# Fused SSM convolution and 32-head attention: another order of projections, shifts and loads in the setup

## The chip, the cores and the metric

One core of one Trainium2 chip runs the whole program in one launch. The metric is device time in microseconds (us), the median of the runs; smaller is better. Engines are named as the profile names them: PE (TensorE matmul), PEld (its weight loads), DVE (VectorE), ACT (ScalarE), POOL (GpSimd), SP (SyncE, which here only issues DMAs).

## The reference

Two unrelated halves, each from an input of 2048 positions by 576 channels, are joined along the channels.

```python
# half a: a diagonal state-space convolution, 576 channels with 128 complex modes each
dt = exp(log_dt); P = exp(dt * A * l)            # A = A_re + i A_im, l = 0..2047
K  = real(einsum("dn,dnl,dn->dl", C, P, dt * B))
a  = irfft(rfft(pad(u)) * rfft(pad(K)))[:2048] + u * Dskip
# half b: attention, 32 heads of 18, one key and one value head shared by all
q = x @ wq; k = x @ wk; v = x @ wv
p = softmax(q k^T * 18**-0.5); o = p v; b = o @ wo
out = concatenate([a, b], axis=-1)
```

## The kernel before

**Attention.** Positions are cut into four chunks of 512 columns (`CT`), keys and queries alike. Transposed scores are made for a pair of heads at a time: a step of the main loop takes one pair, one query chunk and one block of 128 keys. Two matmuls (`scores`, L470) write a tile `s` of 128 x 1024, one ACT instruction (`exponentials`, L478) turns it into `P`, and four matmuls per two of these (`product`, L768) add `P` times the values (`v_sb`) into the bank `ops`. There are 1024 such exponentials. The loop takes them in threes (`NS` = 3 banks of `s`).

The two operands of `scores` are augmented: `kaug` holds, for each key, 18 rows of the rounded key, 18 of its rounding rest, 18 of the rounded key again and a row of ones; `aug` holds for each of a pair of heads the rounded query twice, its rest, and a row (54 or 118) with minus a bound of the scores, so that the exponential needs no maximum. The bound comes from the largest absolute key and query entries: a reduction (`km`, `ab`), a small matmul with `spread` (`kmx`), a product (`aw`), a matmul with `sel` (`up`), a maximum (`un`), and `sh`, which a DMA carries into the row.

Queries come in five groups of output columns per chunk (`MQ`; m = 0 to 4). Group (0, 0) is projected in the setup. The others are projected in pieces between the steps (`qproj`, L347), stored to DRAM (`qd`) by POOL's queue, and fetched by SP as `aug` tiles, five of them in a ring.

**The state-space half** (`Conv`) runs beside it: twelve groups of 48 channels, each with a front (exponentials, sines, tables made by DVE, a matmul `kg`) and a back (transforms by matmuls with `dft`, products on DVE). `arguments` prepares for a group the phases `f`, `r` (cosine and sine) and the exponents `m`; ACT takes the sines and the exponential of them, between two loads of its function table, and DVE multiplies both with `m` (L1072, L1074). In the setup `begin` lets the first group run twelve pieces ahead, up to these two products.

**Order.** PE, ACT and DVE run in the order in which the program writes them. A planner in `main` (class `Clock`, `fill`) writes it: it keeps a model of the engines' times and puts side work (query projections, output projections, transforms) between the steps while a credit lasts. SP's and POOL's orders are set by the scheduler of the language; eight semaphores are used in turn for the DMAs of SP and ACT together, eight for POOL's, so a DMA waits until the eighth before it has landed.

**The setup**, the place of the change. SP loads for each of the five 128-row pieces k of x first the part of chunk 0 (`x0`) and then that of the three other chunks (`xr`). PE projects, piece by piece, the keys of all four chunks into one bank (`kps`, one strip of 32 rows each) and the first query group into another (`q0_0`), then the values (`vps`). Then come the rounding, the DMAs into `kaug` (`place`, chunk by chunk) and `aug` (L405), the bound, the shift row (L444), the other groups' key maxima (`kmx4`), and the values turned by four transposes (`vp`). Only then `main` writes its first scores.

Of the kernel before, what the change touches and what calls it, by code (L numbers as in the profile page):

```python
# [9 lines left out]
F32 = mybir.dt.float32  # L10
# [174 lines left out]
class Attention:  # L185
# [36 lines left out]
    def setup(self, tp, conv):  # L222
# [9 lines left out]
        spread = tp.tile([P, 140], F32, name="spread_sb")  # L232
# [6 lines left out]

        keys = cp.tile([P, 5, CT], F32R, tag="oT", name="keys")  # L240
        kh, kl, vt = keys[:, 0, :], keys[:, 1, :], keys[:, 2, :].bitcast(F32)
        self.q0 = keys[:, 3, :], keys[:, 4, :]
        ident = tp.tile([P, P], F32, name="ident")
        km = tp.tile([P, 5], F32, name="km")
# [4 lines left out]

        def load(q, k):  # L250
            n = DT[k][1]
            q.dma_start(x0[:n, k, :], a["xT"][0, :n, k, :])
            q.dma_start(xr[:n, k], a["xT"][1:4, :n, k, :].rearrange("c p n -> p c n"))
# [8 lines left out]
        nc.scalar.dma_start(spread, a["sel"][:, 45:185])  # L262
        nc.gpsimd.dma_start(ident, a["ident"])
        for b in (54, 118):
            nc.gpsimd.dma_start(self.kaug[b:b + 1, :], a["ones"])
        V.memset(self.v[:, :, DH:], 1.0)
        self.ubound, self.first = None, True
        self.aug = {n: self.ring[n % NAUG] for n in range(64)}
        self.ready, self.od, self.qd = set(), {}, {}
# [4 lines left out]
        conv.begin()  # L274
        kps, self.qps = (self.ps_s.tile([P, 2, CT], F32, tag="s", name=n)[:, 0, :] for n in ("kps", "q0_0"))
        pv = self.ps_o.tile([P, CT], F32, tag="o", name="vps")

        def project(ps, j, k):
            for c in range(NCH):
                nc.tensor.matmul(ps[32 * c:32 * c + 32, :], wkv[:, k, j:j + 32], xr[:, k, c - 1, :] if c else x0[:, k, :],  # L280
                                 start=(k == 0), stop=(k == 4), tile_position=(0, 32 * c))
# [3 lines left out]
        for k in range(2):  # L285
            project(pv, 32, k)
        nc.scalar.activation(kh, kps, AF.Copy)
# [11 lines left out]
        for k in range(2, 4):  # L299
            project(pv, 32, k)  # L300
        self.side_work = side = Stream(self.side(), self.k, 99.0)
        while self.first:
            side.advance()
# [1151 lines left out]
```

## Time and profile before

| | |
|---|---|
| median of 3 runs | 1211.45 us (1211.01 to 1211.5) |
| profiled execution | span 1211.2 us from its first to its last instruction |
| PE | 1142.3 us busy (94%) |
| ACT | 1032.6 us (85%), of which 967.8 in 1024 exponentials |
| DVE | 977.2 us (81%) |
| first exponential of a score | starts at 32.79 us |

Busy times of engines overlap and don't add up. The profile's chain of waits follows the work that ended last back from the end; its shares say through which engine the end was reached. Times in the text are from the start of the span. The runs list no separate time for the profiled execution: the median lies 0.25 us above its span.

### The profile page before, as it was taken

To read this page: it belongs to the slowest core of one execution; us is meant where nothing else is said; L and a number is where in the kernel's file an instruction comes from. 1 tells how busy PE (TensorE), PEld (TensorE's weight loads), DVE (VectorE), ACT (ScalarE), POOL (GpSimd) and SP (SyncE) were. 2 spreads that over 40 slices of the span, in tenths; PEclk is the share of its full clock that TensorE was granted. 3 is DMA by queue.
4 is the path that set the end of the run, shared out by engine and by line. 5 is a ranking of instruction groups with operands and counts; after the bars stand their busy time and mean duration, and the time that the engine had idled before them with its cause. 6 is when DMAs were issued, how large, how long until landed. Compare 5 with 4: busy or idle time off the path is not lost.

```text
span 1211.2 us, 32889 instructions
## 1 busy us (share of the span) xinstructions
PE 1142.3 (94%) x13852; PEld 469.4 (39%) x13852; DVE 977.2 (81%) x1564; ACT 1032.6 (85%) x1091; POOL 118.6 (10%) x210
## 2 busy tenths in 40 slices
PE   5999899999899999999998999999999999999997
PEld 1443333343333344334443333444434334334332
DVE  4769978978997978988877988976997995895823
ACT  2788989888889888898987999888999988988983
POOL 2221210210310000010320000010240000000000
PEclk9899999999999999999999999999999999999999
DMA  7442333122343111223323122122143112012111
GB/s 228 146 138 91 100 106 102 52 82 79 108 134 106 36 65 62 81 80 103 107 71 117 40 92 93 35 81 84 52 132 121 47 36 90 26 51 79 35 41 42
DMA packets 61713, 102.15 MB, mean 84 GB/s; under 512 B 17692, under 2 KB 28570, under 8 KB 61048
## 3 DMA queue, kind: packets, MB, share of 16 engines
q1 hardware_dynamic: 47046, 85.32, 21.2%
q0 software_dynamic: 13824, 14.07, 4.5%
q8 instruction: 111, 1.82, 0.6%
q10 hardware_dynamic: 690, 0.60, 0.2%
q14 instruction: 42, 0.34, 0.1%
HBM read 55.66 MB, written 42.89 MB: 81 GB/s over the span
## 4 chain that ended last, share of the span: by engine, by line
PE 73%; DVE 11%; ACT 8%; issue 3%; DMA 3%; SPq 0%; POOL 0%; ACTq 0%; DVEq 0%
PE ops L768 30%; PE s L470 22%; ACT P L478 8%; PE q L347 5%; PE op L182 4%; PE iy L182 3%; PE kg L1139 3%; DVE acc L112 2%; DMA xr<-xT 2%; DVE ks L112 1%; DVE tab L112 1%; PE hu L182 1%; PE hk L182 1%; PE lu L182 1%; PE lk L182 1%
## 5 line engine op out<-in xcount | busy, mean ns | idle before, releaser
L478 ACT ACTIVATE P<-s 128x1024 f32<-128x1024 f32 x1024 | 967.8, 1031 | 144.7 <-PE s L470 139.9
L768 PE MATMUL ops<-P,v_sb 128*32 128x512 f32 x4096 | 515.4, 599 | 5.6 <-DVE o L116 5.3
L470 PE MATMUL s<-aug,kaug 55*128 55x512 f32 x2048 | 364.0, 442 | 23.8 <-ACT P L478 21.4
L470 PEld LDWEIGHTS s<-aug,kaug 55*128 55x128 f32 x2048 | 169.1, 185 | 331.9 <-ACT P L478 301.1
L768 PEld LDWEIGHTS ops<-P,v_sb 128*32 128x32 f32 x4096 | 114.2, 110 | 155.3 <-issue 120.4
L412 POOL DMA_DIRECT2D qd<-qh x116 | 66.4, 578 | 403.4 <-DVE qh L116 403.4
L347 PE MATMUL q<-x,wq_sb 128*32 128x256 f32 x1360 | 85.7, 389 | 2.9 <-DVE ob L116 1.5
L182 PE MATMUL op<-wo_sb,oT 126*32 126x288 f32 (+1 forms) x1144 | 82.9, 410 | 4.8 <-DVE ob L116 4.1
L112 DVE TENSOR_TENSOR tab<-tab,tt 128x576 f32<-128x576 f32 (+1 forms) x72 | 59.1, 821 | 1.7
L347 PEld LDWEIGHTS q<-x,wq_sb 128*32 128x32 f32 x1360 | 41.1, 111 | 48.0 <-issue 18.6
L112 DVE TENSOR_TENSOR tab<-sum,r 128x576 f32<-128x576 f32 (+1 forms) x72 | 58.7, 816 | 0.0
L112 DVE TENSOR_TENSOR tab<-r,dif 128x576 f32<-128x576 f32 (+1 forms) x72 | 58.7, 816 | 0.0
L112 DVE TENSOR_TENSOR tt<-f,sum 128x576 f32<-128x576 f32 (+1 forms) x72 | 58.7, 816 | 0.0
L112 DVE TENSOR_TENSOR tab<-tab 128x576 f32<-128x576 f32 (+1 forms) x72 | 58.6, 814 | 0.0
L182 PEld LDWEIGHTS op<-wo_sb,oT 126*32 126x32 f32 (+1 forms) x1144 | 32.3, 109 | 50.9 <-issue 18.9
L116 DVE COPY ksb<-kg 128x192 f32<-128x192 f32 x48 | 17.4, 363 | 42.0 <-PE kg L1139 41.7
L112 DVE TENSOR_TENSOR acc<-acc,pt 128x1728 f32<-128x1728 f32 (+2 forms) x36 | 48.6, 1350 | 0.4
L112 DVE TENSOR_TENSOR pt<-us,ks 128x1728 f32<-128x1728 f32 (+2 forms) x36 | 48.0, 1349 | 0.1
L450 POOL DMA_DIRECT2D qd<-sh x19 | 11.8, 619 | 353.6 <-DVE sh L120 353.5
L1139 PEld LDWEIGHTS kg<-tab 128*32 128x32 f32 x2304 | 36.4, 110 | 23.5 <-issue 8.5
L182 PE MATMUL iy<-w,dft_sb 128*32 128x192 f32 x768 | 38.5, 337 | 7.0 <-DVE ql L112 5.9
L112 DVE TENSOR_TENSOR u<-u,iy 128x384 f32<-128x384 f32 x24 | 13.2, 551 | 37.0 <-PE iy L182 36.8
(134 smaller groups left out, 1000.5 us busy)
## 6 DMA issues: line engine op xcount, KB each, us to landing
aug<-qd SPq DMA_DIRECT2D x124, 110.0 KB
od<-o SPq DMA_DIRECT2D x31, 256.0 KB
fr<-stage SPq DMA_DIRECT2D x10, 624.0 KB
qd<-qh POOLq DMA_DIRECT2D x24, 216.0 KB, 4.5
u<-u SPq DMA_DIRECT2D x12, 384.0 KB
kd<-ksb SPq DMA_DIRECT2D x12, 384.0 KB
kt<-kd SPq DMA_DIRECT2D x48, 96.0 KB
outa<-u SPq DMA_DIRECT2D x12, 384.0 KB
```

What stands on the lines that cost most here:

```text
L112: return self.v.tensor_tensor(out, *a, **k)
L116: return self.v.tensor_copy(out, *a, **k)
L182: nc.tensor.matmul(ps[j:e], w[:, j:e], x, start=start, stop=stop, tile_position=(0, j))
L347: nc.tensor.matmul(ps[o, 256 * f:256 * f + 256], w[:, k, i], xt[:, k, x], start=(k == 0), stop=(k == 4), tile_position=(0, 32 * j))
L412: q.dma_start(qd[h:h + n, row + d:row + d + nd, cs], src[i1:i1 + n * nd, :cs.stop - cs.start].bitcast(F32))
L450: q.dma_start(qd[h0 + n0:h1, 54, :].rearrange("p (a n) -> p a n", a=2), two(sh, h1 - h0 - n0))
L470: nc.tensor.matmul(ps[:, j, :], self.kaug[r, kb * P:(kb + 1) * P], t[r, :], start=True, stop=True)
L478: nc.scalar.activation(pt, ps, AF.Exp, scale=SCALE)
L768: nc.tensor.matmul(o_ps[32 * j:32 * j + 32, :], self.v[:, kb, :], pts[2 * n + j // 2][:, j % 2, :], start=(kb == 0), stop=(kb == 15), tile ...
L1139: nc.tensor.matmul(ps[32 * g:32 * g + 32, d, :], t[:, :32], t[:, 32:], start=(j == 0), stop=(j == 1), tile_position=(0, 32 * g))
```

## The change

One pass over chunk 0 now makes the keys of that chunk and the first 96 query columns in one bank (`first`): three strips of queries, one of keys. `xr` is loaded after all of `x0`. A second pass (`rest`) makes the keys of the other chunks and the fourth strip of queries in another bank (`second`), and the values. For the first four heads (two pairs, 32 exponentials) the shift is one number per partition, given to the exponential as its bias, and row 54/118 of their `aug` tiles is set to zero. What came after the values in the setup (transposes of `vp`, `kmx` for all groups, `place` of chunks 2 and 3, the loads of `wq` and `dft`) moves into `settle`, which `main` calls after the first three exponentials. The first group's sine of `f` goes ahead of the keys' copy on ACT, `m` is made later, and `begin` advances 6 and 4 pieces, so the two products with `m` are no longer in the setup. The first group's other queries go to DRAM from POOL (`store_first`) and no longer from SP.

```diff
+        for j in range(2):
+            nc.gpsimd.memset(self.ring[j].bitcast(F32), 0.0)
         conv.early()
         nc.scalar.dma_start(self.wq[0], a["wq"][0])
-        load(nc.sync, 0)
         nc.sync.dma_start(wkv, a["wkv"])
-        for k in range(1, 5):
-            load(nc.sync, k)
-        self.load_wq(1)
+        for k in range(5):
+            nc.sync.dma_start(x0[:n, k, :], a["xT"][0, :n, k, :])
...
+        for k in range(5):
+            nc.sync.dma_start(xr[:n, k], a["xT"][1:4, :n, k, :].rearrange("c p n -> p c n"))
...
+        self.load_wq(1)
...
-        conv.begin()
+        conv.begin(6)
...
+        def rest(k):
+            for c in range(1, NCH):
+                project(p2, c - 1, 0, c, k)
+            queries(p2, 3, k)
             for c in range(NCH):
+                project(pv, c, 32, c, k)
         for k in range(5):
-            project(kps, 0, k)
-            matmul4(nc, self.qps, self.wq[0][:, k, :], x0[:, k, :], start=(k == 0), stop=(k == 4))
...
+            for j in range(3):
+                queries(p1, j, k)
+            project(p1, 3, 0, 0, k)
+        nc.scalar.activation(h1, p1, AF.Copy)
...
+        self.place(0, h1, l1, 96, (nc.sync, nc.sync))
+        for pr in range(2):
+            for row, src in ((0, h1), (18, h1), (36, l1)):
+                for j in range(2):
+                    h, b = 2 * pr + j, 64 * j + row
+                    q = nc.sync if pr and row == 36 else nc.gpsimd
+                    q.dma_start(self.aug[pr][b:b + 18, :].bitcast(F32), src[h * DH:h * DH + DH, :].bitcast(F32))
...
+        conv.begin(4)
+        rest(0)
+        nc.tensor.matmul(small[:, 0:1], spread[:, 0:128], self.km[:, 0:1], start=True, stop=True)
...
+        rest(1)
+        matmul4(nc, small[:, 8:12], aw, self.sel[:, 0:4])
+        V.tensor_reduce(self.bias, small[:, 8:12], axis=AX.X, op=ALU.max)
+        V.tensor_scalar(self.bias, self.bias, -SCALE, None, op0=ALU.mult)
+        for k in range(2, 5):
+            rest(k)
+        V.tensor_copy(h2, p2)
+        V.tensor_tensor(l2, p2, h2.bitcast(F32), op=ALU.subtract)
+        self.place(1, h2, l2, 0, (nc.sync, nc.gpsimd))
+        V.tensor_copy(vt.bitcast(F32), pv)
+        V.tensor_reduce(self.km[:, 4:5], p2, axis=AX.X, op=ALU.max, apply_absolute_value=True)
...
+    def settle(self, conv):
...
+        vp = self.bank(CT, "vp").rearrange("p (j n) -> p j n", j=4)
+        for j in range(4):
+            nc.tensor.transpose(vp[:, j, :], self.vt[:, j * P:(j + 1) * P], self.ident)
+        for src, dst in ((ab[96:, 0:1], ab[96:, 1:2]), (km[96:, 4:5], ab[96:, 0:1]), (ab[96:, 1:2], km[96:, 4:5])):
+            V.tensor_copy(dst, src)
         V.tensor_scalar(km[:, 0:4], spread[:, 136:140], km[:, 4:5], None, op0=ALU.mult)
...
+        conv.start()
+        K.t += 2.0
+        K.v = K.t + 4.0
+        K.fill = K.v
...
-        nc.scalar.activation(pt, ps, AF.Exp, scale=SCALE)
+        if (c, pr // 2) == (0, 0):
+            nc.scalar.activation(pt, ps, AF.Exp, bias=self.bias, scale=SCALE)
+        else:
+            nc.scalar.activation(pt, ps, AF.Exp, scale=SCALE)
...
             s = self.step
+            if r == 0:
+                self.settle(conv)
...
         V.tensor_scalar(r.bitcast(I32), f.bitcast(I32), 0x7FFFFFFF, None, op0=ALU.bitwise_and)
-        yield "v", 0.0, False
+        if k == 0:
+            nc.scalar.activation(f, f, AF.Sin, scale=TWO_PI)
+        yield "v", 0.0, False
+        if k == 0:
+            tt(m, ch(av, NF), row(1), op=mu)
+            yield "v", 0.0, False
...
-            cv.start()
             at.main(cv, flag)
```

What it does to the engines' orders is seen at three places. The first is PE at the end of the setup: the last projections and the first scores (`s_0_0` is head pair 0 with key block 0). Before:

```order
L280 MATMUL vps<-x_123,wkv_sb 32x512
L280 MATMUL vps<-xr,wkv_sb 32x512 x3
L321 MATMUL kmx_319<-km,spread_sb 128x4 x3
L321 MATMUL kmx_319<-km,spread_sb 64x4 x2
L325 MATMUL vp<-ident,keys 128x128 x4
L470 MATMUL s_0_0_352<-aug_111,kaug 128x512 x2
L470 MATMUL s_1_0_355<-aug_112,kaug 128x512 x2
L470 MATMUL s_0_1_358<-aug_111,kaug 128x512 x2
L347 MATMUL q_1_377<-x_123,wq_sb 32x256 x20
L470 MATMUL s_1_1_401<-aug_112,kaug 128x512 x2
```

The same place now:

```order
L280 MATMUL second<-x_124,wq_sb 32x512
L284 MATMUL vps<-x_124,wkv_sb 32x512
L284 MATMUL vps<-xr,wkv_sb 32x512 x3
L485 MATMUL s_0_0_297<-aug_110,kaug 128x512 x2
L485 MATMUL s_1_0_300<-aug_111,kaug 128x512 x2
L485 MATMUL s_0_1_303<-aug_110,kaug 128x512 x2
L341 MATMUL vp<-ident,keys 128x128 x4
L349 MATMUL kmx<-km,spread_sb 128x4 x4
L349 MATMUL kmx<-km,spread_sb 64x4 x2
L485 MATMUL s_1_1_378<-aug_111,kaug 128x512 x2
```

The transposes and the key maxima have gone behind the first three pairs of scores, and twenty matmuls of the second query group, which stood behind these, have gone to a later place. The second place is DVE's opening, before (from the making of `m`):

```order
L112 TENSOR_TENSOR m_152<-raw_127,pos_sb 128x1248
L112 TENSOR_TENSOR f_150<-raw_127,pos_sb 128x1248
L120 TENSOR_SCALAR r_151<-f_150 128x1248
L112 TENSOR_TENSOR f_150<-f_150,r_151 128x1248
L120 TENSOR_SCALAR r_151<-f_150 128x1248
L112 TENSOR_TENSOR r_151<-r_151,m_152 128x1248
L112 TENSOR_TENSOR f_150<-f_150,m_152 128x1248
L124 TENSOR_REDUCE km<-kps 128x1
```

Now, the end of `settle` and the first work of the state-space half in the main loop:

```order
L120 TENSOR_SCALAR km<-spread_sb,km 128x4
L116 COPY v_sb<-vp 128x16x18
L124 TENSOR_REDUCE kmax<-kmx 128x5
L131 MEMSET wq_sb 1x1 x3
L1339 MEMSET dft_sb 1x1
L996 MEMSET u_350 1x1
L996 MEMSET u_355 1x1
L120 TENSOR_SCALAR aw_0_376<-ab_0_196,kmax 128x128
L112 TENSOR_TENSOR r_154<-r_154,m_155 128x1248
L112 TENSOR_TENSOR f_153<-f_153,m_155 128x1248
```

The two products with `m` have moved from before the first reduction of the keys to behind the whole setup. The third place is SP's queue from the loads to the first keys in `kaug`, now:

```order
L255 DMA x_124<-xT 128x512 x4
L255 DMA x_124<-xT 64x512
L260 DMA xr<-xT 128x3x512 x4
L260 DMA xr<-xT 64x3x512
L220 DMA wq_sb<-wq 128x640
L332 DMA kaug<-keys 18x512 x6
L307 DMA aug_111<-keys 18x512 x2
L986 DMA dt_220<-ldt 128x48
L987 DMA raw_219<-prm 128x288
```

Before, `x` and `xr` alternated, and the two loads each of `dt` and `raw` for the next groups stood ahead of the first `kaug` rows; now they stand behind them.

More of the change, by code (lines that the diff above doesn't have):

```diff
@@ L292, in place @@
-        def place(c):
-            for r, t in ((0, kh), (36, kh), (18, kl)):
-                for b in (0, 64):
-                    nc.sync.dma_start(self.kaug[b + r:b + r + 18, c * CT:(c + 1) * CT].bitcast(F32), t[32 * c:32 * c + 18, :].bitcast(F32))
-        place(0)
-        pk = self.bank(4, "kmx")
-        nc.tensor.matmul(pk, spread[:, 0:128], km[:, 0:4], start=True, stop=True)
-        for k in range(2, 4):
-            project(pv, 32, k)
-        self.side_work = side = Stream(self.side(), self.k, 99.0)
```

131 lines of the change are left out of this document (59 added, 72 removed).

## The prediction

> **What bounds the kernel now.** I read the page's parts 1 and 4 first.
>
> ```profile
> PE 1142.3 (94%) x13852; PEld 469.4 (39%) x13852; DVE 977.2 (81%) x1564; ACT 1032.6 (85%) x1091; POOL 118.6 (10%) x210
> PE 73%; DVE 11%; ACT 8%; issue 3%; DMA 3%; SPq 0%; POOL 0%; ACTq 0%; DVEq 0%
> ```
>
> Nearly three quarters of the chain that ended last go through PE, whose 94% leave 69 us without a matmul. ACT is busy almost as long. So time is saved by less work on PE, or by less time in which PE waits. The change takes no projection away, so only the second counts, and its place is the opening. There I read the chain in order of time.
>
> ```profile
> 10.65 11.39 DMA xr<-xT
> 22.18 0.63 PE kps L280 x3
> ...
> 28.02 0.92 PE vps L280 x8
> ...
> 28.99 2.28 DMA aug<-sh
> ...
> 31.66 1.95 PE s L470 x6
> 33.61 4.42 PE q L347 x40
> 38.03 1.03 PE s L470 x6
> ```
>
> The last piece of `xr` lands at 22.04 us (10.65 + 11.39). From there to the first scores pass 9.6 us: the rest of keys and queries, the values, and the DMA of the shift row. The timeline shows ACT and PE behind it; the last row is of a table by windows, whose third column from the end is the granted clock.
>
> ```profile
> 32.79 2.85 ACT L478 ACTIVATE P<-s 128x1024 f32<-128x1024 f32 x3 [8.06 <-PE s L470]
> 38.63 2.86 ACT L478 ACTIVATE P<-s 128x1024 f32<-128x1024 f32 x3 [2.98 <-PE s L470]
> 38.99 2.37 PE L347 MATMUL q<-x,wq_sb 128*32 128x256 f32 x40
> 41.29 0.96 PE L470 MATMUL s<-aug,kaug 55*128 55x512 f32 x6
> 31.60:38.00 6.40, 6.34 (x48) 3.02 (x48) 6.33 (x12) 2.85 (x3) 0.00 (x0) 0.50 0.18 47
> ```
>
> The first three exponentials start at 32.79, the next three at 38.63, since twenty query matmuls stand between (forty executions: a float32 matmul of the program is run as two). PE had half its clock (0.50) there: the forty took 4.42 us, and 2.37 at 38.99; six executions of scores took 1.95, and 0.96 at 41.29.
>
> **The change part by part.** *Loads.* `xr` comes after all of `x0`, with no byte more. The `dt` and `raw` of the next groups, issued while the last `xr` was under way, now come later.
>
> ```profile
> 13.23 0.33 SPq L967 DMA_DIRECT2D raw<-prm  x1
> 17.00:18.00 1.00, 1.00 (x10) 0.15 (x2) 0.00 (x0) 0.99 (x2) 0.00 (x0) 1.00 1.06 216
> 20.00:21.00 1.00, 0.66 (x8) 0.00 (x0) 1.00 (x2) 0.00 (x0) 0.00 (x0) 1.00 1.08 168
> ```
>
> The DMA engines were full (share 1.08) but slow (168 GB/s) ahead of the landing. Two `dt` (128 x 48 numbers, 24 KB) and two `raw` (128 x 288, 144 KB) are 0.34 MB: 1.6 us at 216 GB/s. So the last landing is between 20.4 and, unchanged, 22.04, or 0.6 later if the new order leaves the queues a gap. I take 21.6, nearer to the row.
>
> *From the landing to the first exponential.* Eight matmuls of the last `rest` stand there now.
>
> ```profile
> 6.33 0.36 DVE L112 TENSOR_TENSOR raw<-raw,dt 128x192 f32<-128x192 f32 x1 [5.18 <-DMA raw<-prm]
> 10.05 1.06 PE L280 MATMUL kps<-x,wkv_sb 128*32 128x512 f32 x1 [10.05 <-DMA wkv_sb<-wkv]
> 26.51 0.59 PE L280 MATMUL vps<-x,wkv_sb 128*32 128x512 f32 x1
> 26.94 0.59 PE L280 MATMUL vps<-x,wkv_sb 128*32 128x512 f32 x1
> ```
>
> Four strips run side by side; one execution follows the other after 0.43, so a group of four matmuls takes 0.86 and a `rest` of two groups 1.72. PE can hold this pace: five groups of the first pass and five `rest` are 15 x 0.86 = 12.9 us, and about 2 more for a first stretch at 1.06 an execution; begun when `wkv` and `x0` land, now among the first loads (8 rather than 10.05, estimated: `raw`, issued just ahead of them, had landed by 6.33), they end by 23. From the landing it is 21.6 + 1.72 = 23.3; I take 23.5. PE comes from unbroken work and should have its full clock: first exponential 0.4 to 0.6 later, at 24, 8.8 earlier than 32.79. Bias, first keys and first `aug` rows hang on the first pass, whose loads come before all of `xr`; I cost them at nothing under these loads, and weigh that cover below.
>
> *`settle`.* Values and key maxima now stop PE behind three pairs of scores.
>
> ```profile
> 28.97 0.69 DVE L116 COPY keys<-vps 128x512 f32<-128x512 f32 x1 [0.27 <-PE vps L280]
> 24.63 0.23 DVE L120 TENSOR_SCALAR km<-spread_sb,km 128x4 f32<-128x4 f32 x1
> 30.16 0.66 PE L325 MATMUL vp<-ident,keys 128*128 128x128 f32 x4 [0.28 <-DVE kmax L124]
> 30.85 0.46 DVE L116 COPY v_sb<-vp 128x288 f32<-128x288 f32 x1 [0.75 <-PE vp L325]
> 28.83 1.05 PE L321 MATMUL kmx<-km,spread_sb 128*128 128x4 f32 x10
> ```
>
> The keys' group of the last `rest` ends 0.86 before it, at 22.65. Then come 0.3 to reach DVE, four passes over a bank at 0.69 (2.8), 0.3, `vp` 0.66, 0.15 and the copy 0.46 (the narrow `km` steps, 0.23 and three smaller, lie beside `vp`), 0.3, `kmx` 1.05: 28.7. A pair of scores later the fourth exponential starts at 29.2; before it was 38.63: 9.4 earlier. But the twenty query matmuls (2.37 at full clock) then still lie ahead. At equal work the gain is 9.4 - 2.4 = 7.0.
>
> *What is given back.* The products with `m`:
>
> ```profile
> 18.87 1.46 DVE L112 TENSOR_TENSOR r<-r,m 128x1248 f32<-128x1248 f32 x1 [5.08 <-ACT m L1061]
> 20.25 1.45 DVE L112 TENSOR_TENSOR f<-f,m 128x1248 f32<-128x1248 f32 x1
> 31.29 0.56 DVE L112 TENSOR_TENSOR t<-f,w 128x384 f32<-128x384 f32 x1
> 100.00:150.00 50.00, 44.73 (x496) 17.56 (x486) 45.46 (x71) 44.30 (x48) 12.17 (x20) 0.97 0.35 108
> 950.00:1000.00 50.00, 49.14 (x584) 19.37 (x580) 47.37 (x67) 43.84 (x47) 0.00 (x0) 1.00 0.09 30
> 1150.00:1200.00 50.00, 50.00 (x528) 19.48 (x532) 17.08 (x33) 38.72 (x42) 0.00 (x0) 1.00 0.07 25
> ```
>
> They lay where DVE had idled for 5.08 us, and now fall into its work: 0 to 2.9. DVE is nearly full in some stretches (47.37 of 50) and has 33 us free near the end; I take 0.3. The queries of heads 6 and 7 are projected later while their scores come earlier: before, the same stores went out behind the projection that ended at 41.4 (38.99 + 2.37); put off by up to the 2.37 of these matmuls, they may cost 0 to 2.4; taken 0.3, since that is a wait only if PE reaches the pair first. The memsets, the bias operand and POOL's longer list lie beside other work: 0. Sum 7.0 - 0.6 = 6.4, so 1211.45 - 6.4 = **1205.0 us** for the median; the profiled span, 1211.2, lies 0.25 below it.
>
> *The clock.* Half clock came behind a stretch with little work on PE (28.97 to 31.66: `kmx` and `vp`, 1.7 us), and `settle` makes such a stretch, 23.5 to 28.7 with 0.96 + 0.66 + 1.05 = 2.7 us of matmuls. I charge none, since the old program paid for 6.4 us at half clock too; if the new one pays as before, the scores and products of its second group are 0.96 and 0.9 longer: 1207. The Trainium skill ("TensorE: Matmul & The Clock Gate", Part 1) says that an idle window of about 3.4 us halves the clock and about 3.4 us of steady work restores it. By that rule a stretch of 5.2 us that is half empty may or may not hold an idle window; if it does, the sum is the 1207, if not, the 1205. The rows agree with it that the clock is halved behind a stretch of little work; it came back only after 6.4 us.
>
> **The rivals.** *ACT decides, not PE.* If the put-off matmuls find room where PE waits for ACT, the whole 9.4 stays: 1202. For it: ACT's 1032.6 us are almost as long as PE's. Against: the chain has 8% on ACT.
>
> *The first scores wait for loads.* Each SP DMA waits for the eighth before it, and two `aug` rows of the second pair stand behind the last `xr` and `wq`.
>
> ```profile
> 28.99 0.71 ACTq L444 DMA_DIRECT2D aug<-sh  x1
> ```
>
> 320 KB of `wq` at 200 GB/s (1.6), an issue of 0.7 and the chain's 2.28 to land make 21.6 + 4.6 = 26.2 for that pair instead of 23.9; the copies hide most, and `settle` ends 1.4 later: 1206.4, or 1208 if POOL's rows are late too.
>
> *The sine bursts lie bare* (the rival on the other side). Six times ACT leaves the scores for the sine table.
>
> ```profile
> 132.08 1.28 ACT L1058 ACT_TABLE_LOAD   x1
> 134.15 4.52 PE L347 MATMUL q<-x,wq_sb 128*32 128x256 f32 x80
> 140.31 1.51 PE L182 MATMUL iy<-w,dft_sb 128*32 128x192 f32 x32 [1.63 <-DVE ql L112]
> ```
>
> PE then lives on side work: here 4.52 of queries and two `iy` of 1.51. In the new order the first burst comes twelve exponentials later and has the queries but no `iy` beside it, 3.0 us less cover. One such burst gives 1208; with three the gain of 6.4 is gone, from there on it is slower, and with four it ends at 1217. For it: all six bursts lie elsewhere in the new order. Against: in that order the others keep about as much beside them.
>
> *DVE decides.* Then what counts is when its state-space work begins: `t` at 31.29 before; now 28.7 + 0.9 (maximum, memsets, `aw`) + 2.9 = 32.5. The earlier scores are worth nothing, and it ends 1.2 later: 1212.6, no change. For it: 47.37 of 50. Against: the 33 us free at the end.
>
> That the setup doesn't get shorter at all would need the first pass to wait for `xr`, and its loads don't.
>
> **How the numbers follow.** About 0.2% (2.4 us) can be told from no change. Forecast (1203 to 1207.5) 0.53; ACT 0.13; loads 0.08; one bare burst 0.06; DVE 0.12, of which 0.10 within 2.4 us and 0.02 slower; three and more bare bursts 0.08. Faster is 0.53 + 0.13 + 0.08 + 0.06 = 0.80, same 0.10, slower 0.10. The range goes from ACT's 1202 with the landing at 20.4 (1200.5) to two bare bursts, 1211, which leaves out 0.2.
>
> **What would show it.** First exponential near 24 and the fourth near 29.2, with `kmx` just ahead of it: the sum's first half. First scores waiting for `aug`: the loads. PE idle in the windows around the table loads by more than before (100 to 150: 50 - 44.73 = 5.3 us): the bursts. `t` later than 31.3 and DVE without idle to the end: DVE. A first exponential after 28, or an end later than 1211, proves the forecast wrong.

## The result, and the profile after

The changed kernel takes 1209.74 us (median of 20 runs, 1207.14 to 1212.19), the kernel before, run beside it on the same chip, 1211.47 (20 runs, 1205.77 to 1214.46). The ratio is 0.9991, with a 95% interval of 0.9981 to 1.0002: 1.7 us less, which can't be told from no change. The forecast was 1205.0. The time lies in the forecast's range, but the gain is only a quarter of the 6.4 us forecast.

The profiled execution of the changed kernel has a span of 1206.8 us and took 1208.62; in all its 20 runs the time is 1.7 to 1.9 above the span. So the span of 1211.2 that the prediction worked from belongs to an execution of about 1213, a long one of the kernel before, and the spans (4.4 apart) overstate the gain.

Of the page after, part 1's engines and part 4's chain:

```profile
PE 1140.2 (94%) x13862; PEld 470.7 (39%) x13862; DVE 978.4 (81%) x1570; ACT 1034.8 (86%) x1090; POOL 129.9 (11%) x233
PE 74%; DVE 10%; ACT 9%; issue 4%; DMA 2%; SPq 0%; ACTq 0%; DVEq 0%
```

Span less PE's busy time is 66.6 us without a matmul, against 68.9 before. The timeline of PE after shows where the opening went; a row begins with start and duration, and in brackets stands the idle time ahead and what ended it:

```profile
22.18 0.63 PE L284 MATMUL second<-xr,wkv_sb 128*32 128x512 f32 x3 [1.62 <-DMA xr<-xT]
...
24.89 0.63 PE L284 MATMUL second<-xr,wkv_sb 128*32 128x512 f32 x3 [0.78 <-DMA xr<-xT]
...
27.55 0.81 PE L485 MATMUL s<-aug,kaug 55*128 55x512 f32 x2 [0.74 <-DMA kaug<-keys]
28.76 0.90 PE L485 MATMUL s<-aug,kaug 55*128 55x512 f32 x4 [0.40 <-DMA aug<-keys]
29.59 0.66 PE L341 MATMUL vp<-ident,keys 128*128 128x128 f32 x4
30.80 1.27 PE L349 MATMUL kmx<-km,spread_sb 128*128 128x4 f32 x12 [0.55 <-DVE v_sb L116]
32.00 1.23 PE L485 MATMUL s<-aug,kaug 55*128 55x512 f32 x6
```

The last `rest` waits for `xr` until 24.89 (the prediction had its landing at 21.6); then the first pair of scores waits for a row of `kaug`, and the second for a row of `aug`. From there `vp`, `kmx` and the fourth pair follow in the order forecast. The timeline of ACT:

```profile
28.39 3.19 ACT L494 ACTIVATE P<-s,bias 128x1024 f32<-128x1024 f32 x3 [9.26 <-PE s L485]
32.54 3.13 ACT L494 ACTIVATE P<-s,bias 128x1024 f32<-128x1024 f32 x3 [0.96 <-PE s L485]
35.86 12.21 ACT L494 ACTIVATE P<-s,bias 128x1024 f32<-128x1024 f32 x12 [0.20 <-PE s L485]
```

The first exponential comes at 28.39 (forecast 24), the fourth at 32.54 (29.2). And a dozen exponentials with the bias operand run without a gap, 1.018 us apart; before, six ran 0.943 apart:

```profile
41.83 5.66 ACT L478 ACTIVATE P<-s 128x1024 f32<-128x1024 f32 x6 [0.34 <-PE s L470]
```

The loads by windows (columns as in the prediction: granted clock, DMA share, GB/s last), first before, then after:

```profile
8.00:14.00 6.00, 3.95 (x20) 0.99 (x24) 5.69 (x5) 0.17 (x1) 0.00 (x0) 1.00 1.05 403
```

```profile
8.00:14.00 6.00, 6.00 (x40) 1.39 (x35) 4.15 (x4) 1.24 (x1) 0.00 (x0) 1.00 0.92 307
...
100.00:150.00 50.00, 44.81 (x490) 17.88 (x486) 45.86 (x74) 47.37 (x50) 11.69 (x20) 0.97 0.34 106
```

The loads in another order moved 307 GB/s where 403 went before. The last row is the stretch in which the first sine burst begins: PE is idle for 5.2 us in it, as before (5.3). But it ends in the middle of a wait, which the timeline of PE after shows:

```profile
150.86 1.06 PE L786 MATMUL ops<-P,v_sb 128*32 128x512 f32 x8 [4.07 <-DVE o L116]
```

So take the 22 us around the burst, from 6 us ahead of its first table load, before and then after:

```profile
126.10:148.10 22.00, 18.06 (x212) 8.32 (x216) 19.39 (x29) 19.80 (x20) 4.09 (x7) 0.92 0.29 84
```

```profile
134.50:156.50 22.00, 16.27 (x140) 6.31 (x140) 21.49 (x30) 19.14 (x19) 4.32 (x8) 0.84 0.56 182
```

PE is idle there for 3.9 us before and 5.7 after.

### The profile page after: what moved, and what is told of

Same layout as the page of the kernel before. It is cut to its first block, busy times and chain, and to the rows that moved or that the text cites. A ratio compares the mean times of both kernels' runs of the same rounds, so it can differ in the third digit from the quotient of the medians.

```text
span 1206.8 us, 32948 instructions
## 1 busy us (share of the span) xinstructions
PE 1140.2 (94%) x13862; PEld 470.7 (39%) x13862; DVE 978.4 (81%) x1570; ACT 1034.8 (86%) x1090; POOL 129.9 (11%) x233
## 4 chain that ended last, share of the span: by engine, by line
PE 74%; DVE 10%; ACT 9%; issue 4%; DMA 2%; SPq 0%; ACTq 0%; DVEq 0%
PE ops L786 31%; PE s L485 22%; ACT P L496 7%; PE q L380 5%; PE op L182 5%; PE kg L1166 3%; PE iy L182 3%; DVE acc L112 1%; PE hu L182 1%; PE lk L182 1%; DMA xr<-xT 1%; DVE ks L112 1%; PE hk L182 1%; PE lu L182 1%; PE fin L182 1%
## 5 line engine op out<-in xcount | busy, mean ns | idle before, releaser
L496 ACT ACTIVATE P<-s 128x1024 f32<-128x1024 f32 x992 | 937.9, 1030 | 128.5 <-PE s L485 123.9
L494 ACT ACTIVATE P<-s,bias 128x1024 f32<-128x1024 f32 x32 | 33.0, 1121 | 14.1 <-PE s L485 14.1
L1166 PE MATMUL kg<-tab 128*32 128x64 f32 x2304 | 41.6, 220 | 0.0
L112 DVE TENSOR_TENSOR ks<-ks 128x576 f32<-128x576 f32 (+1 forms) x48 | 41.0, 854 | 0.7
```

What stands on the lines that cost most here:

```text
L112: return self.v.tensor_tensor(out, *a, **k)
L494: nc.scalar.activation(pt, ps, AF.Exp, bias=self.bias, scale=SCALE)
L496: nc.scalar.activation(pt, ps, AF.Exp, scale=SCALE)
L1166: nc.tensor.matmul(ps[32 * g:32 * g + 32, d, :], t[:, :32], t[:, 32:], start=(j == 0), stop=(j == 1), tile_position=(0, 32 * g))
```

## The experiments

Each kernel is the changed one with the edit shown, or another of these kernels where the text says so. All were timed in five rounds (before again in three), beside runs of the kernel before. The table has, from each profiled execution: the start of the last `rest` (the last of the five pieces of the second pass), of the first scores, of the 4th and the 65th exponential (counted in ACT's timeline), and the time from the 65th to the end of the span.

The expectations name theories by letters. A: the loads of the opening land late, by their order (A1) or by a new draw in each execution (A2). B: the end isn't set in the opening. C: the bias operand costs time. D: DVE's time counts. P: the planner's order of the side work counts.

| kernel | ratio to before, 95% | last `rest` | first scores | 4th | 65th | 65th to end |
|---|---|---|---|---|---|---|
| before | | | 31.66 | 38.63 | 105.90 | 1105.3 |
| before again | 0.9997 (0.9976, 1.0019) | | 31.85 | 37.47 | 104.97 | 1106.5 |
| changed | 0.9991 (0.9981, 1.0002) | 24.89 | 27.55 | 32.54 | 103.24 | 1103.5 |
| changed again | 0.9993 (0.9980, 1.0006) | 23.80 | 26.98 | 32.94 | 103.78 | 1103.9 |
| wq late | 0.9981 (0.9966, 0.9995) | 25.72 | 28.57 | 33.40 | 103.86 | 1104.9 |
| x0 pieces | 0.9980 (0.9969, 0.9992) | 23.04 | 25.26 | 30.99 | 101.46 | 1105.7 |
| interleave | 1.0027 (1.0010, 1.0043) | 32.33 | 34.16 | 39.12 | 109.79 | 1105.1 |
| no bias | 0.9978 (0.9966, 0.9991) | 22.53 | 25.06 | 29.94 | 99.54 | 1103.9 |
| bias all | 1.0260 (1.0238, 1.0281) | 22.58 | 25.83 | 30.92 | 102.09 | 1138.2 |
| fill | 1.0000 (0.9983, 1.0018) | 25.92 | 28.63 | 33.98 | 103.55 | 1105.8 |
| delay | 1.0041 (1.0026, 1.0057) | 25.62 | 27.85 | 39.14 | 109.61 | 1107.1 |
| combined | 0.9984 (0.9970, 0.9999) | 22.96 | 27.71 | 33.48 | 103.09 | 1104.6 |
| rows | 0.9956 (0.9939, 0.9972) | 22.95 | 24.77 | 29.73 | 99.44 | 1105.2 |
| products | 0.9941 (0.9922, 0.9960) | 24.59 | 26.50 | 31.40 | 98.44 | 1099.7 |
| products busy | 0.9924 (0.9898, 0.9950) | 24.86 | 27.00 | 32.10 | 99.06 | 1101.8 |
| plan after | 0.9994 (0.9977, 1.0011) | 24.00 | 26.65 | 31.69 | 98.74 | 1108.9 |
| plan products | 1.0022 (1.0008, 1.0037) | 25.86 | 27.72 | 33.72 | 106.26 | 1107.1 |
| rows and products | 0.9890 (0.9863, 0.9917) | 23.15 | 25.68 | 31.84 | 97.87 | 1099.7 |

The first eleven kernels below the two of before deal out the side work in the order of the changed kernel (PE's order is the same), the five with "products" or "plan" do not, so that their 65th exponential has other work behind it. So has that of the two of before: there 64 executions of `hk` and `lk`, 3.5 us of PE, lie ahead of it (from 96.8 us on), which lie behind it in the changed order (from 105.7 us on).

**Does time won in the opening reach the end?** The delay kernel:

```diff
+        idle = self.bank(CT, "idle")
+        for k in range(5):
+            matmul4(nc, idle, self.wq[0][:, k, :], self.x0[:, k, :], start=(k == 0), stop=(k == 4))
         for m in range(2, 5):
```

> The changed kernel, with 40 more executions of matmuls on PE (the first query group once more, its result unused) at the end of settle, ahead of the fourth pair of scores: 4.3 us at full clock, up to 8.6 at half clock, so the fourth exponential starts 4.8 to 9 us later than 32.54. Theories A and C: time in the opening reaches the end one for one, so the end is later by as much as the fourth exponential, 4.8 to 9 us. Theory B: the stream behind makes part of it up, and the end is later by less than half of that.

The timeline of PE in the delay kernel:

```profile
32.66 6.01 PE L182 MATMUL idle<-x,wq_sb 128*32 128x512 f32 x40 [0.28 <-DVE u L999]
38.60 0.96 PE L488 MATMUL s<-aug,kaug 55*128 55x512 f32 x6
```

The fourth exponential came 6.6 us later than 32.54 and the end 6.1 later than the changed kernel (1.0041 against 0.9991). Theory B falls: what the opening loses reaches the end about one for one (the 6.1 is good to some 2 us), though DVE had no more work than before. The rows kernel below shows the same of a gain.

**The loads.** The second weight group put off, x0 in three transfers, the old order of the loads, and both kernels again:

```diff
-        self.load_wq(1)
...
-        for m in range(2, 5):
-            if m < 4:
+        for m in range(1, 5):
+            if 1 < m < 4:
```

> The changed kernel, with the load of the second weight group (wq_1, 320 KB) put off from the loads of the opening to the other weights in settle; PE's, ACT's and POOL's orders are the same. Theory A, the loads of the opening: the changed kernel gained 1.7 us and not 6.4 because the last xr landed at 24.85 instead of 21.6 and the rows of aug and kaug behind it let the first scores go at 27.55 and 28.76; what is won in the opening reaches the end one for one. Then 320 KB less at about 200 GB/s let the last xr land up to 1.6 us earlier, near 23.3, the first exponential comes near 27, and the end 1 to 1.6 us earlier than the changed kernel (ratio to before about 0.9975). Theory B, the opening is not where the end is set: the first exponential comes earlier, the end stays within 0.5 us of the changed kernel. Theory C, the bias operand costs: as B for this run.

```diff
-        for k in range(5):
-            n = DT[k][1]
-            nc.sync.dma_start(x0[:n, k, :], a["xT"][0, :n, k, :])
+        for k0, k1 in ((0, 2), (2, 4), (4, 5)):
+            n = DT[k0][1]
+            nc.sync.dma_start(x0[:n, k0:k1, :], a["xT"][0, :n, k0:k1, :])
```

> The changed kernel, with x0 loaded in three transfers (two of 512 KB, one of 128 KB) instead of five; all other orders are the same. In the changed kernel the DMA engines moved only 277 to 342 GB/s from 8 to 14 us (share 0.83 to 1.01), where before they moved 399 to 409. Theory A: eight transfers in flight of which five are small hold too few bytes; with larger pieces the rate from 8 to 14 us goes back towards 400, 0.4 to 0.6 MB more have landed by 14 us, and the last xr lands 1 to 2.5 us earlier than 24.85, the first exponential 1 to 2 us earlier, the end 1 to 2 us earlier. If the rate stays at 300, the number of transfers is not the cause of the late landing. Theory B: an earlier first exponential, no earlier end. Theory C: no change at the end.

```diff
-        nc.sync.dma_start(wkv, a["wkv"])
         for k in range(5):
             n = DT[k][1]
             nc.sync.dma_start(x0[:n, k, :], a["xT"][0, :n, k, :])
+            nc.sync.dma_start(xr[:n, k], a["xT"][1:4, :n, k, :].rearrange("c p n -> p c n"))
+            if k == 0:
+                nc.sync.dma_start(wkv, a["wkv"])
...
-        for k in range(5):
-            n = DT[k][1]
-            nc.sync.dma_start(xr[:n, k], a["xT"][1:4, :n, k, :].rearrange("c p n -> p c n"))
```

> The changed kernel with the old order of the loads: x0 and xr take turns piece by piece and wkv comes behind the first pair; PE's, DVE's, ACT's and POOL's orders are those of the changed kernel. Theory A1, the new order of the loads costs rate: the 273 to 332 GB/s from 8 to 14 us go back to about 400 as before, the last xr lands at 22 to 22.5, the first pass ends about 3 us later than 14.4 since it waits for the last x0, the rows for kaug and aug follow it, and the first exponential comes at 26 to 27; end 0 to 2 us earlier than the changed kernel. Theory A2, the landing is drawn anew: rate and last landing anywhere in what the others showed (273 to 353 GB/s; 22.5 to 25.7), and the end 0 to 3 us later because of the later first pass.

> The changed kernel once more, beside the others on one chip, for a second profile of the same program. In the runs so far the same loads let PE reach the last rest at 24.89 us (changed kernel), 25.62 (delay) and 22.53 (no bias). Theory A1, the landing is set by the order of the loads: it comes again at 24 to 26. Theory A2, the landing is drawn anew in each execution: anywhere from 22.5 to 26, and with it the first exponential from 26 to 29. Time, by every theory: the ratio to before of 0.9991 again, within 0.0015.

> The kernel before once more, for a second profile. In the changed kernel the last rest came anywhere from 22.5 to 25.7 us with the same loads. Theory A1, the old order of the loads keeps the DMA engines full: 3.9 to 4.1 MB by 14 us, the last xr at 21.5 to 22.5 and the first exponential at 32.3 to 33.3 again. Theory A2, every order scatters alike: the last xr anywhere from 21 to 25, and the first exponential with it. Time: a ratio of 1.000 within 0.002.

Ten profiled executions, besides that of wq late, had x0 in five transfers ahead of xr. Added up from the DMA records, they had moved 3.27 to 3.54 MB by 14 us, and their last `rest` started anywhere from 22.53 to 25.92, at 24.5 on the mean. Putting off wq_1 (3.17 MB) didn't bring it forward: 25.72, a miss of theory A's price for it; that its end is still 1.2 us earlier than the changed kernel's is less than the intervals can tell. With x0 in three transfers, in four executions of four kernels, 3.65 to 3.76 MB had moved, and the last `rest` started at 22.95 to 23.15, in three of them without any wait for `xr` (rows and products waited 0.90 us once): there PE's own pace is the bound. The x0-pieces kernel's fourth exponential came 1.6 us earlier than the changed kernel's, and its end 1.3. Before, 3.99 and 4.01 MB had moved, and the last `xr` released PE at 22.18 both times. The row of the x0-pieces kernel for the stretch of 307:

```profile
8.00:14.00 6.00, 5.12 (x32) 1.52 (x36) 4.20 (x4) 1.25 (x1) 0.00 (x0) 1.00 1.04 353
```

So the order costs rate (theory A1), and as far as these few executions tell it also makes the landing vary (the half of A2 that holds). SP's queue shows what is likely behind it: only x0's first piece, 256 KB, went out at 2.14 us before all eight transfers that may be under way were taken, and the next followed at 5.13; before, 768 KB of `xr` had gone out in that place (2.15). The Trainium skill ("DMA: Bandwidth & Descriptors", Rules for kernel authors) asks for 1 MiB or more in a transfer; the three larger pieces agree with it in direction, and one transfer of 1 MB wasn't tried. The interleaved order brought most of the rate back (369 GB/s from 8 to 14 us, 3.67 MB by 14 us), and yet it is no way back: the first pass waits for x0's last piece until 22.48, and the end comes 4.4 us later than the changed kernel's, where A1 had 0 to 2 us earlier and A2 0 to 3 later.

```profile
22.48 1.07 PE L279 MATMUL first<-x,wq_sb 128*32 128x512 f32 x3 [3.95 <-DMA x<-xT]
```

**The bias operand.**

```diff
-            nc.scalar.activation(pt, ps, AF.Exp, bias=self.bias, scale=SCALE)
+            nc.scalar.activation(pt, ps, AF.Exp, scale=SCALE)
```

> The changed kernel, with the first 32 exponentials taken without the bias operand (the shift of the first four heads is left out there); the bias is still made, and all orders are the same. In the changed kernel these 32 took 1.12 us each, where the others took 1.03, and twelve in a row took 12.21 (1.018 apart) against 5.66 for six (0.943 apart) before. Theory C, the bias operand costs: the 32 go back to 1.03 us, and since ACT runs without a gap in 12 and in 9 of them, the end comes 1 to 2.6 us earlier than the changed kernel. Theory A: the durations may fall but the end stays within 0.5 us, since the landings are unchanged (first exponential at 28.4). Theory B: no change at the end either.

```diff
         else:
-            nc.scalar.activation(pt, ps, AF.Exp, scale=SCALE)
+            nc.scalar.activation(pt, ps, AF.Exp, bias=self.zero, scale=SCALE)
```

> The changed kernel with a bias operand (a column of zeros) on the other 992 exponentials too; all orders are the same. Without the bias the 32 exponentials of the no-bias run took 0.95 us apart and went through exponentials 0 to 64 in 73.5 us, the changed kernel in 74.9. Theory C, the operand costs about 0.08 us in each exponential and ACT is near enough to the path that 32 of them cost 1.4 us: ACT's busy time grows by 992 x 0.08 to 0.09 = 79 to 89 us to about 1115 to 1125, and the end comes 30 to 60 us later (1.4 of 2.6 us reached the clock of the whole in the 32). Theory A and B: each exponential is longer, but ACT has 172 us of idle time, so that the end is later by less than 10 us.

The groups of the page, busy time and mean ns of one behind the bar, first of the changed kernel, then with the operand on all:

```profile
L496 ACT ACTIVATE P<-s 128x1024 f32<-128x1024 f32 x992 | 937.9, 1030 | 128.5 <-PE s L485 123.9
L494 ACT ACTIVATE P<-s,bias 128x1024 f32<-128x1024 f32 x32 | 33.0, 1121 | 14.1 <-PE s L485 14.1
```

```profile
L498 ACT ACTIVATE P<-s,zero 128x1024 f32<-128x1024 f32 x992 | 1021.3, 1121 | 80.9 <-PE s L487 75.1
```

The operand takes 91 ns (1121 - 1030). On all, ACT's busy time grew by 83 us and the end by 33 (1.0260 against 0.9991): 0.03 us of each reaches the end. For the first 32, from the fourth to the 65th exponential it takes 70.5 to 70.8 us with the operand (changed twice, wq late, x0 pieces, interleave, delay) and 69.6 to 69.7 without (no bias, fill, combined, rows): 1.0 us. Theory C holds, at the lower end of the 1 to 2.6 us expected; the no-bias kernel as a whole is 1.6 us faster than the changed one (0.9978 against 0.9991, less than the two intervals can tell apart). The Trainium skill has this price ("ScalarE: Activation LUTs", What ACT_TABLE_LOAD costs): about 93 ns for a pointer operand; the trace agrees, with 91.

**The shift without the operand.** DVE writes it into the aug tiles; `rows` is the old loop over the stores of one row group:

```diff
+        for pr in range(2):
+            for b in (32, 96):
+                V.tensor_scalar(self.aug[pr][b:b + 32, :], self.bias[b:b + 32].broadcast_to([32, CT]), -1.0, None, op0=ALU.mult)
+        rows(18, h1)
+        rows(36, l1)
```

> The changed kernel with the first shift put where the other heads have theirs: four operations of DVE (32 x 512 each) write the negative of the maximum into rows 32 to 63 and 96 to 127 of the first two aug tiles at about 19.3 to 21.3 us, where DVE has no other work; the rows of aug from 18 on are stored behind that, and the first 32 exponentials have no bias operand. Nothing is left out. Theory C: the 32 exponentials go back to 0.95 us apart, exponentials 0 to 64 go back to 73.5 us, and the end comes about 1.4 us earlier than the changed kernel, less up to 1 us if the rows of aug land later (first exponential by more than the landing of xr sets). Theory A: no change but by the landing.

The 69.6 us came back, but this execution drew a late landing (25.92), and the second pair of scores waited 1.08 us for its rows, stored later: 1.0000, no gain. With the loads mended too (x0 in three transfers, wq_1 late), and the next `dt` and `raw` behind these rows:

```diff
-        conv.begin(4)
+        conv.begin(1)
...
+        rows(36, l1)
+        conv.begin(3)
```

> The changed kernel with three edits at once, nothing left out: x0 in three transfers, wq_1 loaded in settle, and the first shift written into the aug tiles (as in the fill run) instead of a bias operand; the loads of the next dt and raw go behind the last two rows of aug on SP. PE's order is that of the changed kernel. If the missing gain sits in the landing of xr, in the rows of kaug and aug behind the loads, and in the bias operand, then 3.7 MB or more have moved by 14 us (3.2 to 3.5 with five transfers), the last rest starts at 22.5 to 23.5, no score waits for kaug or aug by more than 0.5 us, the fourth exponential starts at 30 to 31, exponentials 4 to 64 take 69.6 us instead of 70.7, and the end comes 2.5 to 3.5 us earlier than the changed kernel: ratio to before 0.9965 to 0.9975. If these things only looked like the cause: 0.999 again.

The landing (3.68 MB, 22.96) and the exponentials from the fourth to the 65th (69.6 us) did as expected. But the scores waited, and since the rows of `aug` are issued ahead of the transfers that the profile names, these rows are what came last:

```profile
27.71 0.47 PE L490 MATMUL s<-aug,kaug 55*128 55x512 f32 x1 [2.85 <-DMA dt<-ldt]
```

POOL issued six rows from 20.75 on (the next expectation says eight), the last at 24.41. The rows kernel gives two of them to ACT, behind three pieces of `conv`:

```diff
-                    q = nc.sync if pr and row == 36 else nc.gpsimd
+                    q = (nc.scalar, nc.sync)[pr] if row == 36 else nc.gpsimd
...
+        rows(36, l1, (1,))
+        conv.begin(3)
+        rows(36, l1, (0,))
```

> The combined kernel, whose last rest started at 22.96 us but whose first scores waited until 27.71 for the last rows of aug (POOL stored eight of them one behind the other from 20.75 to 24.9 us), with two of these rows stored by ACT instead of POOL; nothing is left out. If the rows were what held the scores, the first scores go at 25 to 26 us, the fourth exponential starts at 30 to 31.5, and the end comes 2 to 3.5 us earlier than the changed kernel (ratio to before 0.996 to 0.9975), as the forecast of the opening would have it. Rival: the rows are held by the transfers under way, not by POOL's order: first scores after 27 again, ratio 0.998 to 0.999.

PE, then ACT, in its timeline:

```profile
24.77 1.77 PE L491 MATMUL s<-aug,kaug 55*128 55x512 f32 x6
26.81 0.63 PE L347 MATMUL vp<-ident,keys 128*128 128x128 f32 x4 [0.27 <-DVE km L124]
27.99 1.27 PE L355 MATMUL kmx<-km,spread_sb 128*128 128x4 f32 x12 [0.55 <-DVE v_sb L116]
29.19 1.15 PE L491 MATMUL s<-aug,kaug 55*128 55x512 f32 x6
```

```profile
25.74 2.85 ACT L500 ACTIVATE P<-s 128x1024 f32<-128x1024 f32 x3 [5.76 <-PE s L491]
29.73 2.85 ACT L500 ACTIVATE P<-s 128x1024 f32<-128x1024 f32 x3 [1.14 <-PE s L491]
```

No score waits, the fourth exponential starts at 29.73, and the end is 5.3 us earlier than before (0.9956 of 1211.86; interval 3.4 to 7.4). With its loads, rows and shift mended the change does what was forecast of it, 6.4, within the interval. PE's order is that of the changed kernel, so the 4.2 us between the two (0.9956 against 0.9991, good to some 2 us) come from these edits.

**The products, and the order of the side work.**

```diff
         for k in range(2, 5):
             rest(k)
+        conv.begin(2)
```

> The changed kernel with the two products with m back in the setup, where DVE has nothing to do (from 19.3 to 26 us), so that t starts 2.9 us earlier than 35.4; the planner then deals out the side work a little otherwise. The prediction charged 0.3 us for having them in the loop. If that is right, or if it is nothing, the end stays within 0.5 us of the changed kernel (ratio 0.9985 to 0.9995). Rival, DVE decides: what counts is when its state-space work starts, and the end comes 2.9 us earlier (ratio 0.997).

It gained 6 us over the changed kernel, twice all the DVE time concerned, and none of the theories had that. The planner, whose model of DVE (`K.v` is where it starts) has other numbers then, deals the side work out in another order. Four more kernels tell the two apart:

```diff
+        if n0:
+            nc.vector.memset(self.spread, 0.0)
+            for _ in range(4):
+                nc.vector.tensor_tensor(self.spread, self.spread, self.spread, op=ALU.mult)
```

> The products kernel with 3 us of other work on DVE where the changed kernel has the two products (a memset and four products of 128 x 512 into a tile that nothing reads, behind the first aw), unknown to the planner: all orders are those of the products kernel, and DVE is as busy as in the changed kernel. Theory D, DVE's time is what the products kernel saved: the end goes back up by 3 to 6 us (ratio 0.9965 to 0.999). Theory P, the planner's other order saved it: the end stays at that of the products kernel (ratio 0.9925 to 0.9955).

```diff
-        K.v = K.t + 4.0
+        K.v = K.t + 1.25
```

> The changed kernel with one constant of the planner changed (the time at which it takes DVE to be free after settle: 1.25 us behind PE instead of 4.0). The work is the same and the products stay in the loop; only the order in which side work is dealt out differs. Theory P, the order is worth as much as the forecast effects: the end moves by more than 2 us from the changed kernel, to either side, likely towards the products kernel since its plan also starts 2.75 us earlier (0.994 to 0.997). Theory D: it stays at 0.999, since DVE has the same work.

```diff
+        conv.begin(2)
...
-        K.v = K.t + 4.0
+        K.v = K.t + 5.5
```

> The products kernel with that constant at 5.5 instead of 4.0 us: the same work and the products in the setup, another order. Theory P: the end moves by more than 2 us from the products kernel, likely up (0.996 to 1.001). Theory D: it stays within 1 us of 0.994.

The rows and the products kernel in one:

> The rows kernel (0.9956) and the products kernel (0.9941) in one: the loads in time, no bias operand, the two products in the setup; nothing is left out, PE's order is that of the products kernel. If the gains lie in different places (opening: 4 us less than the changed kernel up to exponential 64; products: less idle time of PE behind exponential 64), they add: ratio 0.990 to 0.992. If the products kernel gained by the same opening, the two don't add: ratio 0.994 to 0.995.

Two pages' spans and engines, products, then plan products:

```profile
span 1198.1 us, 32945 instructions
...
PE 1136.8 (95%) x13862; PEld 468.7 (39%) x13862; DVE 976.7 (82%) x1571; ACT 1035.0 (86%) x1090; POOL 129.3 (11%) x233
```

```profile
span 1213.3 us, 32959 instructions
...
PE 1140.3 (94%) x13862; PEld 471.1 (39%) x13862; DVE 977.8 (81%) x1573; ACT 1035.5 (85%) x1090; POOL 130.6 (11%) x233
```

With the same work and the products in the same place, PE is idle for 61.3 us in the one order and 73.0 in the other, and the ratios are 0.9941 and 1.0022, 9.8 us apart. (The spans are further apart, since the profile of the products kernel is of the shortest of its twelve runs, 1199.88 with a median of 1205.27.) Three more us of DVE work in the order of the products kernel took nothing away that the ratios show (0.9924, where D expected at least 0.9965). In the two profiles the busy kernel is 2.6 to 3.1 us later from the 129th exponential on, so that a part of these three us isn't ruled out. So theory D falls with its 3 to 6 us, and P holds: the order is worth as much as all that the prediction counted, to either side. That the plan-after kernel stayed at 0.9994, where 0.994 to 0.997 was thought likely, says that its order happens to be worth what the changed kernel's is: PE idle for 67.9 us (span 1207.7, PE 1139.8) against 66.6. Which piece of an order makes the difference wasn't found, but two profiles narrow it. Products busy and plan after have as much work for DVE and, up to the 336th exponential, nearly the same order of PE; at the 337th they are 0.2 us apart. From there to the 501st (415 to 597 us in products busy) their orders differ, and plan after loses 7.2 us.

By their ratios the two gains add: rows and products is 13.3 us below before (0.9890; 10 to 17), the lowest of all. The profiles don't show how: its fourth exponential starts at 31.84, no earlier than in the products kernel (31.40), and the two end within 0.5 us of each other, though the one is near its median (1199.44, 1199.99) and the other far below.

## Why the prediction was wrong, step by step

- *The last `xr` landing, 21.6 (20.4 to 22.04, 0.6 more for a gap).* This step failed. It took bytes out of a full queue and kept the rate; the new order itself lowered the rate (307 and 324 GB/s from 8 to 14 us, against 403 and 405) and left the DMA engines less full (share 0.92 and 0.96, against 1.05 and 1.06). The last `rest` began at 24.89 and 23.80; before, the last `xr` released PE at 22.18. The "gap" was the right thing and three to four times too small (0.6, against 2.7 and 1.6).
- *PE's pace: five `rest` by 23.* Where no load is waited for, the last one starts at 22.5 to 23.1 and ends, with the forecast's own 1.72, at 24.2 to 24.8. The matmuls of `small` between the first two `rest` and the wait for DVE ahead of them were left out: in the rows kernel they take 0.9 us (16.8 to 17.7). The step is 1 us short, which the landing hides.
- *Bias, first keys and first `aug` rows at nothing.* Wrong; the prediction weighed it only as a rival, at 1.4 us with a chance of 0.08: in the changed kernel the scores wait 0.74 and 0.40, on the second profile 1.26. A row stored under the loads lands 7.5 us behind its issue (median of POOL's ten after), 2.6 before (eight). Landing and rows together put the fourth exponential at 32.54 and 32.94 instead of 29.2.
- *`settle`, 6.55 us from the end of the second group to the fourth exponential.* It looks right, 6.6 from 25.95 (25.32 + 0.63) to 32.54, but by luck. In the second profile it is 8.1 (24.86 to 32.94), with `kmx` and the scores at half clock from 29.8 on. Where no score waits it is 5.8 (rows, 23.97 to 29.73; interleave, 33.37 to 39.12). So the step was priced 0.8 too long, and in the first profile the waits of the scores, which stand ahead of `vp` on PE, made up for it.
- *The bias operand at nothing.* Wrong: 1.0 us. The prediction looked for what hides the making of the bias, not at what it does to an exponential.
- *At equal work, and one for one to the end.* The delay reached the end whole. But the work is not equal at the 65th exponential: the changed order has 3.5 us of `hk` and `lk` still ahead there. From then on, the ten executions of the changed order at normal exponentials take 1103.5 to 1107.1 us, the two of before 1105.3 and 1106.5, so the work put off isn't seen at the end; what hides it stays open.
- *The products at 0.3 (0 to 2.9).* Within it: three us of DVE work at that place did no harm that the ratios show, and at most the 2.6 to 3.1 of one pair of profiles. DVE decides (0.12) falls with it. The queries put off were charged the other 0.3, and from 30 to 110 us after, one score waits 0.3 for a DMA and no other matmul does.
- *The clock, none charged.* The opening's time at half clock was 6.8 and 3.4 us before, 3.4 and 6.8 after: as assumed, on the mean.
- *The sine bursts bare (0.14).* It came in part. The sign that the prediction named, 100 to 150 us, shows 5.2 us idle against 5.3, but it cuts the burst's wait off. In the 22 us around the first burst PE is idle for 5.7 and 7.1 us (two profiles), against 3.9 and 3.9: 1.8 to 3.1 more, where the rival charged 3.0. Around all six it is 19.7 and 20.8 against 17.7. Yet from the 65th exponential to the end PE is idle for 52.9 and 53.8 us in all, against 55.4 and 55.3, so other stretches have less. So the rival saw a part of something larger: an order's worth, some 10 us between two orders of the same work, had no term and no bound.
- *ACT decides (0.13).* Not seen: the time is far from 1202, and with 83 us more on ACT the end moved by 33. But ACT isn't free either, as those 33 show.

The sum anew, with the means of two profiles each: the fourth exponential from 38.05 to 32.74, 5.3 earlier; less 2.4 of query matmuls, 2.9; less 1.0 for the operand: 1.9 us. Measured: 1.7. The forecast of 7.0 - 0.6 missed 3.5 in the landing and the rows (32.74 instead of 29.2) and 1.0 in the operand. It took 0.6 too much from its one profile of before (38.63 instead of 38.05), and charged 0.6 for two terms that the times can't tell from nothing. That the sum meets the measured time so closely is luck in part: it leaves out the 3.5 us put off, the 2 to 3 us more idle time at the bursts, and whatever else the new order is worth. What the runs do show is the rows kernel: in the same order of PE, the loads, rows and shift mended bring back 4.2 of the 4.7 us that were missing. (The range's lower end was added up a little low: 1202 less the 1.2 of the landing is 1200.8, not 1200.5.)

## What to carry to other kernels

When loads are put in another order, don't keep the rate of the old one: look at how many transfers may be under way, and what each then holds, and take the time of small stores under full queues from such a stretch, not from an empty one. Compare a stretch before and after around the same event, not between the same two times. Ask of each operand that is added to an instruction in the inner loop what it costs there. Where a planner deals out side work, a change of its inputs draws a new order, whose worth (here some 10 us between two orders of the same work) can be larger than the edit's: hold the order fixed, or time several, before a gain or a loss is put down to the edit.

## What the hardware showed that was not expected

The granted clock falls to a half in pieces of 3.4 us (records of 3.413 and 6.827 us), and does so around the sine bursts too, and now and then elsewhere (645.8 us before): four to eight such pieces of 3.4 us from the 65th exponential to the end, not the same number in each execution. A piece is worth up to 1.7 us of PE's time, so two more or fewer make 3.4 us, about as much as runs of one kernel differ from their median. The twelve runs of the products kernel go with their mean granted clock: 1199.88 us at 0.990, 1207.38 at 0.982. The stretch of the fourth exponential after the change, with the clock third from the end:

```profile
32.00:34.00 2.00, 2.00 (x14) 0.68 (x14) 1.88 (x10) 1.46 (x2) 2.00 (x5) 0.63 0.41 111
34.00:36.00 2.00, 2.00 (x14) 0.78 (x6) 1.97 (x3) 1.80 (x3) 1.07 (x3) 0.52 0.32 86
```

And ten executions whose programs issue the same first loads on the same queues, small transfers first, began their last `rest` up to 3.4 us apart.
